# Attention and two gated layers on one core: first batch's exponentials head by head on ACT, pooled q and k by products, 32-bit low words, and a table of urgencies for the list schedule

## The chip, the core and the metric

The kernel runs on one core of one Trainium2 chip. The core has a matrix engine (PE, whose weight loads are shown apart as PEld), a vector engine (DVE), a scalar engine (ACT), a general engine (POOL), and a queue engine (SP) that issues every transfer of this kernel. Each works through its own instructions in order, and semaphores join them. The metric is the time of one execution in microseconds, as the median of several runs.

## The reference

Four batches with 8 heads, 576 positions and 64 values a head go through two attentions that are added: a pooled one, in which q, k and v are averaged over groups of 4 positions, and a local one, in which a position sees its neighbours up to distance 3. The sum, as 2304 tokens of 512 values, goes through a product of two projections and a third one, and then through a layer with a leaky rectifier whose slope is `alpha`:

```
q_d = q.reshape(B, H, Sd, 4, D).mean(axis=3)          # k_d, v_d alike
out_up = repeat(sm_attn(q_d, k_d, v_d), 4)
mask = abs(pos[:, None] - pos[None, :]) < 4
out_local = softmax(where(mask, scale * q @ k.T, -1e9)) @ v
x = tokens(out_up + out_local)
x = (x @ w_a) * (x @ w_b) @ w_out
h = x @ w_in;  return (maximum(h, 0) + alpha * minimum(h, 0)) @ w_out2
```

q, k and v are 32-bit floats; the five weight matrices come as 64-bit floats.

## The kernel before

**Attention.** The tokens are cut into 24 tiles of 96 (`TQ`), six to a batch. For a tile, `turn` transposes q and k on PE (four transposes of 128 columns each into one bank of PSUM), ACT copies them to SBUF (`zone`), and DVE sums groups of four columns of the copy into the pooled q and k of the batch (`gq_z`, `gk_z`). `soft` makes the scores of 8 heads in two banks (4 heads, 416 columns each), and per bank DVE takes the maximum of each row and head (`nm`), and subtracts it while it writes the scores to SBUF; then one ACT instruction makes the exponentials of all 832 columns, DVE sums them per head (`nz`), inverts the sums and multiplies. `p_turn` transposes the result, `av_t` multiplies by v, `x_add` adds the pooled attention and splits x into two 16-bit parts (`xt`). `g_top`, `g_minus`, `g_exp` and `g_out` are the pooled attention of a batch; it needs the pooled q and k of all six tiles.

**Weights.** `narrow` makes 32-bit floats out of 64-bit ones, in halves: ACT scales the low word down and writes it into the low 16 bits of the place it was read from, DVE masks the 16 bits above, DVE shifts the high word into the destination, POOL adds the two. Then the weights are scaled and split into two 16-bit parts by ACT and DVE (`wab` for w_a and w_b, `wo` for w_out, and in `zone`, once attention is over, w_in and w_out2).

**Dense layers.** `s1` (24 PE instructions of 288 columns in two groups of 12; then ACT, DVE, ACT, DVE), `s2`, `s3` and `s4` are the dense products. They form the list `chain`, whose order on PE is fixed.

**Order.** The class `Plan` records every operation with a modelled duration (`cost`), and `schedule` lays them out: of the operations that are ready on an engine, the one with the highest `prio` goes first, which is the modelled length of what hangs on it plus a `bias` given by hand for its group (a tile, a chunk of weights, a block). `fill` then puts idle products of an identity matrix (`m<-idf`, 256 columns) into the gaps that PE has by that plan up to 200 us: a number that covers 0.7 of the gap. The names `turn3`, `soft3`, `wab1`, `s1_0_5` are the groups. So a change of costs or biases moves operations on all engines, and the number of fills with them. In the trace nearly everything has the line L269 (the helper that issues), so groups are told by operation and tile.

Of the kernel before, what the change touches and what calls it, by code (L numbers as in the profile page):

```python
# [12 lines left out]
U32 = mybir.dt.uint32  # L13
I64 = mybir.dt.int64
ACTF = mybir.ActivationFunctionType
ALU = mybir.AluOpType
AX = mybir.AxisListType
# [8 lines left out]
class Plan:  # L26
# [66 lines left out]
    def cost(self, eng, method, out, ins, kw):  # L93
        n = self.free(out)
        if eng == self.PE:
            if method == "transpose":
                n = self.free(out)
                w = 2 if ins[0].dtype == F32 else 1
            else:
                w = 4 if ins[0].dtype == F32 else 1  # L100
            return max(0.03, n * w * 0.000425)
        m = max([n] + [self.free(a) for a in ins])
        if eng == self.POOL:
            return 0.2 + m * (0.0026 if method == "tensor_tensor" else 0.0011)
        if eng == self.ACT:
            if ins and ins[0].dtype == U32:
                return 0.2 + 0.00243 * m
            return 0.2 + 0.0009 * m + (0.19 if kw.get("accum_out") is not None else 0)
        if out.dtype == I16:
            return 0.1 + 0.00144 * m  # L110
        if method in ("tensor_scalar", "tensor_copy", "memset", "tensor_scalar_mul"):
            return 0.12 + 0.0009 * m
        return 0.14 + 0.0011 * m
# [79 lines left out]
    def schedule(self, chain):  # L193
        for a, b in zip(chain, chain[1:]):
            b.preds.add(a)
        for o in self.ops:
            for p in o.preds:
                p.succ.append(o)
        for o in reversed(self.ops):
            t = 0.0  # L200
            for s in o.succ:
                t = max(t, s.tail + self.lat(o, s))
            d = o.dur + (sum(o.dma) if o.dma else 0.0)
            o.tail = t + d
            o.prio = max([o.tail + o.bias] + [s.prio + self.lat(o, s) + d for s in o.succ])
            o.left, o.est = len(o.preds), o.free
        ready = {e: [] for e in (self.PE, self.DVE, self.ACT, self.POOL, self.SP)}
        free = dict.fromkeys(ready, 0.0)
        self.dma_free = 0.0
        for o in self.ops:  # L210
            if not o.left:
                ready[o.eng].append(o)
        order = []
        while True:
            best = None
            for e, lst in ready.items():
                if lst:
                    t = max(free[e], min(o.est for o in lst))
                    if best is None or t < best[0]:
                        best = (t, e)  # L220
            if best is None:
                break
            t, e = best
            o = max((o for o in ready[e] if o.est <= t + 1e-9), key=lambda o: (o.prio, -o.n))
            ready[e].remove(o)
            o.start, free[e] = t, t + o.dur
            o.end = free[e]
            if o.dma:
                self.dma_free = max(self.dma_free, t + 0.5) + o.dma[0]
                o.end = max(o.end, self.dma_free + o.dma[1])  # L230
            order.append(o)
            for s in o.succ:
                s.est = max(s.est, o.end + self.lat(o, s))
                s.left -= 1
                if not s.left:
                    ready[s.eng].append(s)
        assert len(order) == len(self.ops)
        self.order = order
        return order
# [36 lines left out]
def kernel(  # L276
# [17 lines left out]
    P = Plan(nc)  # L294
# [3 lines left out]
    def T(method, *a, **kw):  # L298
        P("tensor", method, *a, **kw)

    def V(method, *a, **kw):
        P("vector", method, *a, **kw)

    def A(method, *a, **kw):
        P("scalar", method, *a, **kw)

    def G(method, *a, **kw):
        P("gpsimd", method, *a, **kw)
# [18 lines left out]
    TQ = 96  # L327
    WK = 104
    TPB = S // TQ
# [4 lines left out]
    TP = TQ // FAC  # L334
    H2 = H // 2
    XR = 3 * N1
    scale = 1.0 / float(D) ** 0.5
# [12 lines left out]
    def bank(tag):  # L350
        nbank[tag] += 1
        return banks[tag][(nbank[tag] - 1) % len(banks[tag])]
# [80 lines left out]
    cal = []  # L433
# [26 lines left out]
    def narrow(raw, dst):  # L460


        w = raw.bitcast(I32).rearrange("p (n t) -> p n t", t=2)
        h = raw.bitcast(I16).rearrange("p (n t) -> p n t", t=4)
        A("activation", out=h[:, :, 0], in_=raw.bitcast(U32).rearrange("p (n t) -> p n t", t=2)[:, :, 0],
          func=ACTF.Copy, scale=2.0 ** -29)
        V("tensor_scalar", out=h[:, :, 1], in0=h[:, :, 3], scalar1=-0x4000, scalar2=None, op0=ALU.bitwise_and)
        d = dst.bitcast(I32)
        V("tensor_scalar", out=d, in0=w[:, :, 1], scalar1=3, scalar2=0x3FFFFFFF,
          op0=ALU.logical_shift_left, op1=ALU.bitwise_and)  # L470
        G("tensor_tensor", out=d, in0=d, in1=w[:, :, 0], op=ALU.add)
# [60 lines left out]
    pool_m = const.tile([WK, 3, 120], F32, name="pool_m")  # L532
# [25 lines left out]
    def raw_of(i):  # L558
        r = raw_t(i)
        return (r[:TQ, :H * D], r[:, H * D:2 * H * D], r[:, 2 * H * D:].rearrange("p (h d) -> p h d", h=H))  # L560
# [37 lines left out]
    def win(i):  # L598
        b, t = divmod(i, TPB)
        s0 = t * TQ  # L600
        kb = min(max(s0 - 4, 0), S - WK)
        return b, s0, kb, s0 - kb


    sm = {}

    def load(i, js=(0, 1, 2)):
        b, s0, kb, off = win(i)
        t = raw_of(i)
        for j in js:  # L610
            src, r0, n = ((q, s0, TQ), (k, kb, WK), (v, kb, WK))[j]
            dma(t[2] if j == 2 else t[j].rearrange("p (h d) -> p h d", h=H),
                src[b, :, r0:r0 + n, :].rearrange("h p d -> p h d"))

    def turn(i, tag):

        b, s0, kb, off = win(i)
        rq, rk, _ = raw_of(i)
        qz, kz = qk_of(i)
        t = i % TPB  # L620
        for src, n, dst, acc, o in ((rq, TQ, qz, gq_z[b % 2], 0), (rk, WK, kz, gk_z[b % 2], off)):
            ps = bank(tag)[:, :H2 * n].rearrange("p (a n) -> p a n", a=H2)
            with pe():
                for p in range(H2):
                    T("transpose", ps[:, p], src[:, p * 128:(p + 1) * 128], idf[:n, :n])
            A("copy", dst, ps)
            V("tensor_reduce", out=acc[:, :, t * TP:(t + 1) * TP],
              in_=dst[:, :, o:o + TQ].rearrange("p a (n r) -> p a n r", r=FAC), axis=AX.X, op=ALU.add)

# [10 lines left out]
    def p_of(i):  # L640

        return raw_t(i)[:TQ, :H * WK].rearrange("p (h n) -> p h n", h=H)

    def soft(i, tag="a"):

        qz, kz = qk_of(i)
        m, z = (ring(f"n{x}", [TQ, H]) for x in "mz")
        pss = [bank(tag)[:TQ, :H2 * WK].rearrange("p (h n) -> p h n", h=H2) for _ in range(2)]
        p = p_of(i)
        with pe():  # L650
            for ps in pss:
                T("matmul", ps, idb[:TQ, :TQ], mask[:, win(i)[3] // 4].unsqueeze(1).to_broadcast([TQ, H2, WK]),
                  start=True, stop=False)
            for h in range(H):
                T("matmul", pss[h % 2][:, h // 2], qz[rows(h), h // 2], kz[rows(h), h // 2], start=False,
                  stop=(h >= H - 2))
        for g in range(2):
            hs = slice(H2 * g, H2 * g + H2)
            V("tensor_reduce", out=m[:, hs], in_=pss[g], axis=AX.X, op=ALU.max)
            V("tensor_tensor", out=p[:, hs], in0=pss[g], in1=m[:, hs].unsqueeze(2).to_broadcast([TQ, H2, WK]),  # L660
              op=ALU.subtract)
        A("activation", out=p, in_=p, func=ACTF.Exp, scale=scale)
        V("tensor_reduce", out=z, in_=p, axis=AX.X, op=ALU.add)
        V("tensor_scalar_add", z, z, 1e-9)
        V("reciprocal", z, z)
        V("tensor_tensor", out=p, in0=p, in1=z.unsqueeze(2).to_broadcast([TQ, H, WK]), op=ALU.mult)
# [419 lines left out]
    for f in range(F1):  # L1086
        c, e = divmod(f, FPC)
# [28 lines left out]
    for n, i in enumerate((3, 4, 5)):  # L1116
        t = head_end + 4 * n
# [8 lines left out]
    for b in range(1, B):  # L1126
        for t in range(TPB):
            i = b * TPB + t
            ti = first[b] + pace[b] * t
            bias = lead[b] + spread[b] * (TPB - t)  # L1130
# [15 lines left out]
    for i in range(3, NTILE):  # L1146
        b, t = divmod(i, TPB)
# [27 lines left out]
    for j in range(NBLK):  # L1175
# [6 lines left out]
        for t in range(NB // 128):  # L1182
            on(n0 + 31.6 + 10.3 * t, lambda j=j, t=t: s4(j, t), f"s4_{j}_{t}")

    cal.sort(key=lambda x: x[:2])
    for _, _, fn, P.name, P.bias, P.rel in cal:
        fn()
    P.schedule(chain)
    ib = idf.bitcast(BF16)
# [33 lines left out]
```

## Time and profile before

| | |
|---|---|
| runs | 1040.88, 1047.79, 1048.54 us, median 1047.79 |
| the profiled execution | 1049.7 us, of which the span from the first to the last instruction is 1047.4 |
| PE busy | 1011.8 us (97%), of which 53.4 us are fills |
| DVE busy | 599.8 us (57%) |
| ACT busy | 506.8 us (48%) |
| POOL busy | 133.7 us (13%) |
| mean granted clock of PE | 0.984 |

A row of the page gives an engine's busy time, its share of the span and its instructions. A busy PE is not always useful: the fills count as busy, and two records stand for one product of 32-bit floats. What bounds the kernel has to be read stretch by stretch.

### The profile page before, as it was taken

To read this page: it belongs to the slowest core of one execution; us is meant where nothing else is said; L and a number is where in the kernel's file an instruction comes from. 1 tells how busy PE (TensorE), PEld (TensorE's weight loads), DVE (VectorE), ACT (ScalarE), POOL (GpSimd) and SP (SyncE) were. 2 spreads that over 40 slices of the span, in tenths; PEclk is the share of its full clock that TensorE was granted. 3 is DMA by queue.
4 is the path that set the end of the run, shared out by engine and by line. 5 is a ranking of instruction groups with operands and counts; after the bars stand their busy time and mean duration, and the time that the engine had idled before them with its cause. 6 is when DMAs were issued, how large, how long until landed. Compare 5 with 4: busy or idle time off the path is not lost.

```text
span 1047.4 us, 18866 instructions
## 1 busy us (share of the span) xinstructions
PE 1011.8 (97%) x7749; PEld 701.3 (67%) x7749; DVE 599.8 (57%) x1247; ACT 506.8 (48%) x955; POOL 133.7 (13%) x128
## 2 busy tenths in 40 slices
PE   8889799989999999999988999999999999999998
PEld 5677677768787787887866777754645545454553
DVE  5899998847655567473998577450513315142240
ACT  3677688533433434253766666460624417153350
POOL 2335640001100012000253210000000000000000
PEclk9889999989999999999999999999999999999999
DMA  9674641014310144111661411010010100100000
GB/s 160 226 209 144 163 134 26 1 25 72 72 48 1 48 75 91 24 64 41 205 196 55 151 42 35 13 32 21 11 46 16 41 21 8 66 12 11 21 1 30
DMA packets 95942, 69.50 MB, mean 66 GB/s; under 512 B 71152, under 2 KB 78704, under 8 KB 95856
## 3 DMA queue, kind: packets, MB, share of 16 engines
q1 hardware_dynamic: 95856, 68.31, 24.6%
q8 instruction: 60, 0.98, 0.4%
q14 instruction: 26, 0.21, 0.1%
HBM read 58.86 MB, written 9.44 MB: 65 GB/s over the span
## 4 chain that ended last, share of the span: by engine, by line
PE 84%; DVE 10%; SPq 2%; ACT 2%; issue 1%; DMA 1%; DVEq 0%; ACTq 0%
PE m L269 73%; PE a L269 10%; DVE zone L269 3%; SPq L269 2%; DVE wo L269 2%; DVE wab L269 1%; PE r L269 1%; ACT zone L269 1%; DMA zone<-in_v_dram 1%; DVE nz L269 1%; DVE xt L269 1%; ACT wo L269 0%; DVE gt L269 0%; DVE gm L269 0%; DVE tm L269 0%
## 5 line engine op out<-in xcount | busy, mean ns | idle before, releaser
L269 PEld LDWEIGHTS <-wab 128*128 128x128 f16 x3168 | 306.8, 98 | 166.4 <-issue 10.1
L269 PE MATMUL m<-xt,wab 128*128 128x288 f16 x2304 | 295.6, 286 | 8.0 <-DVE x2s L269 3.9
L269 PE MATMUL m<-xt,zone 128*128 128x384 f16 x1152 | 188.2, 326 | 0.0
L269 PE MATMUL m<-zone,wab 128*128 128x512 f16 x864 | 187.7, 379 | 0.0
L269 DVE SCALAR_TENSOR_TENSOR gt<-tm,nal,tm 128x384 f32<-128x384 f32 x96 | 59.3, 618 | 218.6 <-ACT tm L269 218.6
L269 PEld LDWEIGHTS <-zone 128*128 128x128 f16 x1152 | 112.7, 98 | 74.9
L269 ACT ACTIVATE tm<-m 128x384 f32<-128x384 f32 (+1 forms) x224 | 97.8, 478 | 112.1 <-PE m L269 112.1
L269 PEld LDWEIGHTS <-wo 128*128 128x128 f16 x1152 | 112.0, 99 | 31.2 <-issue 2.7
L269 POOL TENSOR_TENSOR zone<-zone 72x256 f32<-72x256 f32 (+2 forms) x60 | 75.5, 1266 | 393.7 <-DMA zone<-in_v_dram 220.2
L269 PE MATMUL m<-gt,wo 128*128 128x288 f16 x864 | 114.1, 290 | 0.4 <-DVE gt L269 0.3
L269 ACT ACTIVATE zone<-zone 96x832 f32<-96x832 f32 (+4 forms) x69 | 78.2, 1144 | 35.7 <-DVE zone L269 28.3
L269 PE MATMUL a<-zone 64*96 64x104 f32 (+3 forms) x1232 | 86.7, 269 | 4.7 <-DVE zone L269 3.8
L269 ACT ACTIVATE gt<-m,uf 128x512 f32<-128x512 f32 x18 | 12.4, 688 | 157.1 <-PE m L269 157.1
L269 PEld LDWEIGHTS a<-zone 64*96 64x96 f32 (+3 forms) x1232 | 71.3, 154 | 22.7 <-issue 13.6
L269 ACT COPY zone<-a 104x384 f32<-104x384 f32 (+3 forms) x112 | 50.0, 484 | 38.2 <-PE a L269 37.7
L269 ACT COPY tm<-m 128x288 f32<-128x288 f32 x96 | 38.4, 400 | 56.4 <-PE m L269 51.7
L269 DVE SCALAR_TENSOR_TENSOR tm<-m,tm 128x288 f32<-128x288 f32 x96 | 43.5, 453 | 37.7 <-PE m L269 27.6
L269 DVE SCALAR_TENSOR_TENSOR wab<-gt,kap,wab 128x384 f16<-128x384 f32 x96 | 58.8, 612 | 6.3 <-ACT wab L269 6.3
L269 ACT ACTIVATE wab<-gt,kap 128x384 f16<-128x384 f32 x96 | 59.1, 616 | 1.1 <-DVE gt L269 1.1
L269 PE MATMUL m<-idf 128*128 128x256 bf16 x377 | 53.4, 293 | 0.0
L269 ACT ACTIVATE gt<-tm 128x288 f16<-128x288 f32 x72 | 31.6, 442 | 40.8 <-DVE tm L269 40.8
L269 DVE TENSOR_SCALAR zone<-zone 128x512 int16<-128x512 int16 (+3 forms) x48 | 45.0, 964 | 4.2 <-ACT zone L269 3.9
(166 smaller groups left out, 933.3 us busy)
## 6 DMA issues: line engine op xcount, KB each, us to landing
zone<-in_moe_w_in_dram SPq DMA_DIRECT2D x8, 1024.0 KB
zone<-in_moe_w_out_dram SPq DMA_DIRECT2D x16, 512.0 KB
wo<-in_moe_w_a_dram SPq DMA_DIRECT2D x6, 1024.0 KB
wo<-in_moe_w_b_dram SPq DMA_DIRECT2D x6, 1024.0 KB
x_d<-x2s SPq DMA_DIRECT2D x8, 576.0 KB
out_dram<-gt SPq DMA_DIRECT2D x18, 256.0 KB
zone<-in_k_dram SPq DMA_DIRECT2D x21, 208.0 KB
zone<-in_v_dram SPq DMA_DIRECT2D x21, 208.0 KB
```

Source lines behind the costliest of these rows:

```text
L269: f(*args, **kw)
```

## The change

Five edits:

- In `narrow`, ACT writes the low word as 32 bits instead of 16; DVE's write of the upper 16 bits follows as before. The planner's cost of this operation goes from 2.43 to 1.2 ns an element.
- For the tiles of batch 0 (`i < 1 * TPB`) `soft` no longer subtracts on DVE: DVE multiplies the maxima by `-scale`, and ACT reads the scores from PSUM, eight instructions of 104 columns for a tile, each with the maximum as its bias and with the sum of its exponentials as a second result. DVE's sum over the tile goes.
- For batches 0 and 1 (`EARLY = 2`) `turn` no longer sums groups of four on DVE: after the four transposes PE multiplies the same columns by a matrix of ones (`pool_m`, 24 columns), into the rest of the same bank, and ACT copies the 96 columns of sums.
- Every group gets a number from the table `URGENT` on top of its bias.
- The schedule's second half becomes a method of its own, with no effect on the order.

```
@@ Plan.cost
             if ins and ins[0].dtype == U32:
-                return 0.2 + 0.00243 * m
+                return 0.2 + 0.0012 * m
@@ narrow
-        A("activation", out=h[:, :, 0], in_=raw.bitcast(U32).rearrange("p (n t) -> p n t", t=2)[:, :, 0],
+        A("activation", out=w[:, :, 0], in_=raw.bitcast(U32).rearrange("p (n t) -> p n t", t=2)[:, :, 0],
           func=ACTF.Copy, scale=2.0 ** -29)
@@ turn
-            ps = bank(tag)[:, :H2 * n].rearrange("p (a n) -> p a n", a=H2)
+            full = bank(tag)
+            ps = full[:, :H2 * n].rearrange("p (a n) -> p a n", a=H2)
+            sums = full[:, H2 * n:H2 * (n + TP)].rearrange("p (a n) -> p a n", a=H2)
+            early = b < EARLY
             with pe():
                 for p in range(H2):
                     T("transpose", ps[:, p], src[:, p * 128:(p + 1) * 128], idf[:n, :n])
+                if early:
+                    for p in range(H2):
+                        T("matmul", sums[:, p], src[:, p * 128:(p + 1) * 128], pool_m[:n, o // 4, 48:48 + TP],
+                          start=True, stop=True)
             A("copy", dst, ps)
+            if early:
+                A("copy", acc[:, :, t * TP:(t + 1) * TP], sums)
+                continue
             V("tensor_reduce", out=acc[:, :, t * TP:(t + 1) * TP],
@@ soft
             V("tensor_reduce", out=m[:, hs], in_=pss[g], axis=AX.X, op=ALU.max)
-            V("tensor_tensor", out=p[:, hs], in0=pss[g], in1=m[:, hs].unsqueeze(2).to_broadcast([TQ, H2, WK]),
-              op=ALU.subtract)
-        A("activation", out=p, in_=p, func=ACTF.Exp, scale=scale)
-        V("tensor_reduce", out=z, in_=p, axis=AX.X, op=ALU.add)
+            if i < 1 * TPB:
+                V("tensor_scalar_mul", m[:, hs], m[:, hs], -scale)
+                for h in range(H2):
+                    c = H2 * g + h
+                    A("activation", out=p[:, c], in_=pss[g][:, h], func=ACTF.Exp, scale=scale, bias=m[:, c:c + 1],
+                      accum_out=z[:, c:c + 1])
+            else:
+                V("tensor_tensor", out=p[:, hs], in0=pss[g], in1=m[:, hs].unsqueeze(2).to_broadcast([TQ, H2, WK]),
+                  op=ALU.subtract)
+        if i >= 1 * TPB:
+            A("activation", out=p, in_=p, func=ACTF.Exp, scale=scale)
+            V("tensor_reduce", out=z, in_=p, axis=AX.X, op=ALU.add)
@@ end of the kernel
+    URGENT = {"alphas": 35, "bs0": -45, "bs1": -5, "gexp0": -70, "gexp1": -5, "gexp2": 25, "gexp3": -50,
...
-    for _, _, fn, P.name, P.bias, P.rel in cal:
+    for _, _, fn, P.name, bias, P.rel in cal:
+        P.bias = bias + URGENT.get(group(P.name), 0.0)
         fn()
```

Counted over the whole program, the fills go from 377 to 334, 96 products with `pool_m` come in, 24 of the 48 sums of four on DVE go, with 12 subtractions and 6 sums of exponentials, and 12 small multiplications come in.

**DVE, third tile.** These rows of DVE stand in the first part of the program, around the softmax of tile 2, whose scores lie in the banks `a_69` and `a_67` and whose exponentials lie in `x2s`; `wab<-wo` and `wo<-wo` are steps of `narrow`. Before:

```order
L269 TENSOR_REDUCE nm_125<-a_69 96x4
L269 COPY gt_135<-a_68 24x144
L269 TENSOR_TENSOR x2s<-a_69,nm_125 96x416
L269 TENSOR_REDUCE nm_125<-a_67 96x4
L269 TENSOR_REDUCE tr_119<-r_70 2x1
L269 TENSOR_TENSOR x2s<-a_67,nm_125 96x416
L269 TENSOR_SCALAR td_121<-idf,tr_119 2x2
L269 TENSOR_SCALAR wab<-wo 128x1024
```

and now:

```order
L272 TENSOR_REDUCE nm_125<-a_69 96x4
L272 COPY gt_135<-a_68 24x144
L272 TENSOR_SCALAR nm_125<-nm_125 96x4
L272 TENSOR_REDUCE nm_125<-a_67 96x4
L272 TENSOR_SCALAR wab<-wo 128x1024
L272 TENSOR_SCALAR nm_125<-nm_125 96x4
L272 TENSOR_REDUCE tr_119<-r_70 2x1
```

The two subtractions are gone, two multiplications of 4 columns stand in their place, and a step of `narrow` has moved up between them.

**ACT, the same tile.** These rows of ACT stand around the exponentials of tile 2; `wo<-wo` is the low word of a chunk of weights, `zone<-a` with 72 rows is `g_exp` of batch 0. Before:

```order
L269 ACTIVATE wo<-wo 128x1024
L269 ACTIVATE zone<-a_68 72x432
L269 ACTIVATE x2s<-x2s 96x832
L269 ACTIVATE zone<-a_69 72x432
L269 ACTIVATE wo<-wo 128x1024
L269 ACTIVATE zone<-a_67 72x432
```

and now:

```order
L272 ACTIVATE wab,wm_117<-wab 128x1024
L272 ACTIVATE x2s,nz_127<-a_69,nm_125 96x104 x4
L272 ACTIVATE x2s,nz_127<-a_67,nm_125 96x104 x4
L272 ACTIVATE wo<-wo 128x1024
L272 ACTIVATE zone<-a_68 72x432
L272 ACTIVATE zone<-a_69 72x432
```

One instruction has become eight, they read PSUM, and they now stand ahead of `g_exp` of batch 0.

**PE, a tile of batch 1.** These rows of PE stand where the `s1` groups (`m<-xt,wab`) already follow each other; `a<-idf,zone` are the transposes of a tile's k (104 columns) and q (96). Before:

```order
L269 MATMUL a_68<-idf,zone 128x104 x4
L269 MATMUL a_67<-idf,zone 128x96 x4
```

and now:

```order
L272 MATMUL m_65<-xt,wab 128x288
L272 MATMUL a_68<-zone 64x96 x8
L272 MATMUL a_67<-idf,zone 128x104 x4
L272 MATMUL a_67<-pool_m,zone 128x24 x4
L272 MATMUL a_69<-idf,zone 128x96 x4
L272 MATMUL a_69<-pool_m,zone 128x24 x4
```

Behind each four transposes stand four products of 24 columns. Of the twelve such fours of batch 1, two stand ahead of the last long rows of fills and ten behind them. Behind the eighth group of 12 products of `s1`, 30 of the fills stood in the program, and 17 do now.

## Rows read from the trace of the kernel before

**Rows 1.** The page: busy us, share of the span, instructions.
```profile
PE 1011.8 (97%) x7749; PEld 701.3 (67%) x7749; DVE 599.8 (57%) x1247; ACT 506.8 (48%) x955; POOL 133.7 (13%) x128
```

**Rows 2.** Busy time by stretch: stretch, us, PE, PEld, DVE, ACT, POOL, clock, DMA share, GB/s.
```profile
0.00:26.70 26.70, 21.90 (x169) 15.48 (x169) 15.73 (x36) 9.93 (x18) 7.79 (x44) 1.00 0.99 164
26.70:120.60 93.90, 79.45 (x730) 63.17 (x731) 87.45 (x144) 63.91 (x76) 43.70 (x21) 0.87 0.64 186
120.60:200.00 79.40, 79.27 (x744) 63.18 (x744) 70.75 (x164) 59.37 (x116) 21.06 (x16) 1.00 0.28 75
200.00:240.00 40.00, 35.81 (x315) 27.39 (x313) 21.86 (x57) 15.62 (x30) 0.00 (x0) 0.87 0.08 17
240.00:505.00 265.00, 265.00 (x2527) 212.00 (x2526) 164.00 (x392) 102.74 (x219) 21.22 (x25) 1.00 0.27 59
505.00:640.00 135.00, 126.73 (x1017) 99.28 (x1015) 108.92 (x222) 94.36 (x164) 39.96 (x23) 1.00 0.35 114
```

**Rows 3.** Instruction groups of PE: the fills in 26.7:120.6, then in 120.6:200.
```profile
L269 PE MATMUL m<-idf 128*128 128x256 bf16 x296 | 40.6, 293 | 0.0
...
L269 PE MATMUL m<-idf 128*128 128x256 bf16 x30 | 4.1, 273 | 0.0
```

**Rows 4.** The chain of work, 20 to 120 us: start, length, what.
```profile
20.63 6.08 DMA zone<-in_v_dram
...
30.05 2.41 ACT wo L269
...
117.88 1.26 ACT wo L269
...
120.56 5.92 PE m L269 x47
```

**Rows 5.** Instruction groups of DVE in 26.7:120.6 (busy, mean ns); the last in the whole run.
```profile
L269 DVE TENSOR_SCALAR wo<-wo 128x1024 int16<-128x1024 int16 x12 | 16.3, 1359 | 0.1
L269 DVE TENSOR_SCALAR wab<-wo 128x1024 int32<-128x1024 int32 x12 | 9.8, 817 | 0.0
L269 DVE TENSOR_TENSOR zone<-a,nm 96x416 f32<-96x416 f32 x8 | 4.3, 579 | 0.0
L269 DVE TENSOR_REDUCE nz<-zone 96x8 f32<-96x832 f32 x3 | 3.0, 989 | 0.0
L269 DVE TENSOR_REDUCE zone<-zone 128x96 f32<-128x384 f32 x2 | 1.1, 538 | 0.0
...
L269 DVE TENSOR_SCALAR nz<-nz 96x8 f32<-96x8 f32 x24 | 6.0, 249 | 0.1
```

**Rows 6.** Instruction groups of ACT: six in 26.7:120.6, the last two in the whole run.
```profile
L269 ACT ACTIVATE wo<-wo 128x1024 int16<-128x1024 uint32 x12 | 30.1, 2505 | 0.0
L269 ACT ACTIVATE wab<-wab 128x1024 bf16<-128x1024 f32 x6 | 6.3, 1053 | 7.0 <-DVE wab L269 5.0 <-POOL wab L269 2.0
L269 ACT ACTIVATE x2s<-x2s 128x512 int16<-128x512 uint32 x3 | 4.1, 1372 | 0.0
L269 ACT ACTIVATE zone<-zone 96x832 f32<-96x832 f32 x4 | 3.6, 893 | 0.5 <-DVE zone L269 0.4
L269 ACT ACTIVATE xt<-zone,sx 128x384 f16<-128x384 f32 x5 | 2.9, 612 | 0.1
L269 ACT ACTIVATION_READ_ACCUMULATOR wab<-wab 128x1 f32 x6 | 1.1, 188 | 0.0
...
L269 ACT ACTIVATE tm<-m 128x384 f32<-128x384 f32 x192 | 84.3, 488 | 63.1 <-PE m L269 63.1
L269 ACT COPY zone<-a 128x288 f32<-128x288 f32 x8 | 3.2, 399 | 7.8 <-PE a L269 7.5
```

**Rows 7.** The chain of work at 137 and 236 us: small 32-bit products on PE.
```profile
137.49 0.31 PE r L269 x2
...
236.28 2.07 PE a L269 x32
```

**Rows 8.** The chain of work at 540 us, and PE's longest wait in 505:640.
```profile
540.80 3.00 ACT zone L269 x3
...
544.04 2.42 ACT zone L269
...
PE m L269 <- DVE x2s L269: 3.9, 3, 2.3
```

**Rows 9.** The chain of work around 230 us: groups of 12 products of `s2`.
```profile
224.49 3.00 PE m L269 x12
...
234.81 1.47 PE m L269 x12
```

More of the change, by code (lines that the diff above doesn't have):

```diff
@@ L198, in schedule, with reschedule @@
                 p.succ.append(o)
+        return self.reschedule()
+    def reschedule(self):
         for o in reversed(self.ops):
@@ L605 @@
     sm = {}
+    EARLY = 2
     def load(i, js=(0, 1, 2)):
@@ L1183, with group @@
             on(n0 + 31.6 + 10.3 * t, lambda j=j, t=t: s4(j, t), f"s4_{j}_{t}")
+    def group(name):
+        kind = name.rstrip("0123456789")
+        n = name[len(kind):]
+        if kind in ("turn", "bound", "soft", "pturn", "av", "v", "x", "load") and n:
+            b = int(n) // TPB
+            return f"{kind}@{b}" if kind in ("x", "load") else f"t@{b}" if b else f"t0@{n}"
+        if name[:3] in ("s1_", "s2_"):
+            return f"{name[:2]}@{name[3]}"
+        return kind if kind in ("wow", "wos", "wo2w", "wo2s") else name
+    URGENT = {"alphas": 35, "bs0": -45, "bs1": -5, "gexp0": -70, "gexp1": -5, "gexp2": 25, "gexp3": -50,
[12 rows of a table added]
     cal.sort(key=lambda x: x[:2])
-    for _, _, fn, P.name, P.bias, P.rel in cal:
+    for _, _, fn, P.name, bias, P.rel in cal:
+        P.bias = bias + URGENT.get(group(P.name), 0.0)
         fn()
```

12 rows, old and new, of the table URGENT are left out of this document.

## The prediction

> **What bounds the kernel now.** The page comes first [rows 1]: PE is busy 97% of the span. That says that PE ends most of the time, not that it works: 53.4 us are fills, and 1047.4 - 1011.8 = 35.6 us are idle. So I read the stretches next [rows 2], and in each ask who has no time left. From 240 to 505 us PE is busy all 265 us: nothing that DVE or ACT saves there shows, and each product that PE gets shows in full. The same holds from 120.6 to 200 (79.27 of 79.40). From 26.7 to 120.6 it is otherwise: DVE is busy 87.45 of 93.90 us, and PE's 79.45 hold 40.6 us of fills [rows 3]. The chain of waits agrees: up to 26.7 us it hangs on the load of v [rows 4], from there to 120.56 us, where the first long row of `s1` begins, it is DVE nearly throughout, with two low words of `narrow` on ACT in it (2.41 and 1.26 us). From 505 to 640 PE lacks 135.0 - 126.7 = 8.3 us; it waits for DVE most [rows 8], and the chain goes through ACT for 3.00 and 2.42 us there, low words again.
>
> So there are two currencies. Up to 120 us a microsecond of DVE is worth about one, behind that one of PE is.
>
> **The change, part by part.** *Softmax of batch 0.* In the stretch that DVE bounds lie the tiles 2 to 5. Eight subtractions at 579 ns [rows 5] go (4.6 us) and four sums of exponentials at 989 ns (4.0 us); eight small multiplications come. The nearest row to these is an operation on 8 columns, at 249 ns: 2.0 us. Tiles 0 and 1 lie ahead of 26.7 us, where the load of v decides and DVE is busy 15.73 of 26.70 us [rows 2]: nothing.
>
> *Pooled q and k, on DVE.* Two of the 24 sums of four lie in that stretch (538 ns each, 1.1 us, [rows 5]). Twelve lie ahead of it and the other ten behind it, beside a busy PE: nothing. So DVE's stretch gets shorter by 4.6 + 4.0 + 1.1 - 2.0 = **7.7 us**. The bounds: nothing, if another engine takes DVE's place, and some 12 us if the new order also moves DVE's work behind the first `s1`.
>
> *Pooled q and k, on PE.* 96 products come in. 56 of them stand among fills and cost nothing as long as fills stand around them, else their own time. Forty, ten fours, stand in the `s1` rows, where PE has no time left. The trace has no 32-bit product of 24 columns with 128 weight columns. From below I take 32 records in 2.07 us [rows 7], two records a product (72 weight columns, 65 columns moved): 0.13 us. From above a lone product with 128 weight columns and one or two columns moved, 0.31 us, with PE's start on it. Four in a row share a start, so I take 0.17, nearer to the lower row: 40 x 0.17 = **6.8 us later** (5.2 to 12.4).
>
> The Trainium skill has a rule for this: TensorE: Matmul & The Clock Gate, section LDWEIGHTS, lets a load of weights last as many cycles of 1.2 GHz as it has columns, 107 ns for 128. By it a product with two loads would cost 0.21 us, forty 8.5 us, and the sum below would come out 1.7 us later. No run here shows such a product yet.
>
> *ACT's part.* A head's exponentials: 288 columns take 399 ns and 832 take 893 [rows 6], so 104 take about 0.23; an operand by partition adds 612 - 488 = 0.12, the sum read out 0.19: 0.54 us, or 0.44 where neighbours overlap. Eight take 3.5 to 4.3 us, against 0.9. For four tiles in the stretch ACT gets 10 to 14 us more. It had 30 us idle there [rows 2], so this costs nothing on the path while ACT is not late; the last small sum of a tile does come 2.6 to 3.4 us later, and what waits for it on DVE are the reciprocal and the product of the tile, behind which DVE has steps of `narrow` to do.
>
> *Low words.* Sixteen lie in the stretch, 12 of 1024 words at 2505 ns (30.1 us, [rows 6]) and four of 512 at about 1370. Why they are slow the trace does not tell: the same ACT writes 1024 16-bit results side by side in 1053 ns; a 16-bit write at a step of 8 bytes costs DVE 1359 ns against 817 for a 32-bit one side by side [rows 5]; and this is the only ACT row that reads unsigned words. Between no gain and 1053 I take half, about 1.3 us. Most of that is beside the path; on it are 2.41 + 1.26 us [rows 4], halved: **1.8 us** gained (0 to 2.2). From 505 to 640 us half of 5.4 us would be 2.7; DVE, which is waited for there, gains nothing by it, so I take **1.5** (0 to 2.7).
>
> *The order.* It shows 13 fewer fills behind the eighth `s1` group, where PE is the bound. A fill there takes 4.1 / 30 = 0.137 us [rows 3]: **1.8 us** gained. The other thirty that go stand where DVE decides: nothing. The stall of `s1` from 505 to 640 has the same DVE work in front of it in the new order, a little earlier and more spread; I count nothing for that, with 8.3 us as its end. From 200 to 240 us the operations stand as before; nothing.
>
> *The sum.* -7.7 + 6.8 - 1.8 - 1.5 - 1.8 = **-6.0 us**. The profiled execution has 1047.4 us of span and 2.3 around it, 1049.7, and would become 1043.7. It lies 1.9 us above the median of the three runs, 1047.79, which are 0.7% apart among themselves. From the median the same sum gives **1041.8 us**.
>
> **The rivals.** *More comes out of it (1026 to 1036).* The table puts DVE's work in an order in which the first `s1` comes the full 12 us earlier, and the stall at 505 to 640 goes (8.3 us), with products at the lower price: -12 - 8.3 - 1.8 - 1.8 + 5.2 = -18.7, **1029**. For it: both stalls are waits behind DVE operations that could stand later, and the subtractions read PSUM while POOL adds. Against it: DVE's sum up to 640 us falls by little more than the terms above.
>
> *ACT takes DVE's place (slower).* The low words are no faster, and ACT gets 17 us of exponentials (32 x 0.54) less 3.6 and some 1 us of copies: 63.9 + 14.7 = 78.6 us in a stretch in which DVE then has 87.45 - 7.7 = 79.8. From there on both engines are full and wait for each other at each tile: the reciprocal stands behind eight exponentials, and these behind a low word of 2.5 us. At 3.4 us a tile, four tiles pay 13.6: -7.7 + 13.6 + 6.8 - 1.8 = +10.9, **1058.7**. It decides as soon as a low word of 1024 stays above about 2.2 us. For it: nothing in the rows says that the width of the write is what is slow. The Trainium skill speaks for it too: SBUF — State Buffer, section Door 1, lets a step cost nothing as long as two accesses fall into one line of 16 bytes, and a step of 8 bytes does so with 16 bits as with 32. Against that page stands DVE's row, dearer at just that step.
>
> *PE pays more behind 120 us (slower).* Products at 0.31 us are 12.4 us. And PE's clock can fall beside small products: a group of 12 of `s2` took 3.00 us at 224 us, 1.47 at 234 [rows 9], in a stretch with a granted clock of 0.87 [rows 2], after waits and small 32-bit products. If 10 us between 120 and 200 went at 1.2 GHz, 5 us would be lost: -7.7 + 12.4 + 5 - 5.1 = +4.6, **1052**.
>
> *The head does not get shorter:* the loads or POOL's adds (43.7 us in the stretch) set the pace once DVE does not; then the pace of `s1` stays and only PE's terms count: 6.8 - 1.8 = +5.0, less 1.5: **1051**.
>
> **How the numbers follow.** About 1% (10.5 us) is what runs that are 0.7% apart can tell from no change; so faster means below 1037.3, slower above 1058.3. Forecast, 1035 to 1048: 0.46. More comes out of it: 0.26. ACT takes DVE's place: 0.12, PE pays more: 0.09, the head stays: 0.07. Faster: 0.26 and a fifth of the forecast, 0.36. Slower: half of ACT's case and a third of PE's, 0.09, and 0.03 for both at once: 0.12. The rest, 0.52, is within 1%. The range is 1027 to 1056: it leaves out 0.09 below, where more comes out of it than worked out, and 0.1 above.
>
> **What would show each step.** DVE's subtractions of batch 0 gone and its stretch up to the first long row of `s1` 6 to 9 us shorter: the start of that row near 111 us. The low word of 1024 near 1.3 us; at 2.5 ACT's busy share up to there rises above 80%, and DVE, which had no idle time, waits for ACT. The products of 24 columns: a four in 0.5 to 0.9 us between two `s1` groups, and PE's busy time without fills up by 14 to 20 us. From 505 to 640 us, PE's idle time of 8.3 us down to about 7, or to nothing in the first rival. The prediction is wrong if the first `s1` row begins as before, if it begins earlier than 105 us, or if a product with `pool_m` takes over 0.3 us.

## The result, and the profile after

| | median, us | runs, us | ratio to before, 95% interval |
|---|---|---|---|
| before | 1047.38 | 1040.88 to 1048.54 | |
| changed | 1058.76 | 1056.42 to 1060.74 | 1.0117 [1.0098, 1.0137] |

Slower by 11 us, where 6 us less was forecast and 1056 was the range's upper end. The profiled execution took 1057.83 us, of which the span is 1056.1. The page's row of busy times, to set beside [rows 1]:

```profile
PE 1030.2 (98%) x7898; PEld 722.6 (68%) x7898; DVE 586.0 (55%) x1217; ACT 478.3 (45%) x1069; POOL 142.0 (13%) x128
```

PE is busy 18.4 us longer and idle 9.7 us less: the kernel is longer by the difference. The same stretches as in [rows 2] (stretch, us, PE, PEld, DVE, ACT, POOL, clock, DMA share, GB/s):

```profile
0.00:26.70 26.70, 22.35 (x120) 18.82 (x121) 4.01 (x13) 7.07 (x27) 7.73 (x44) 1.00 1.00 166
26.70:120.60 93.90, 80.94 (x775) 63.65 (x773) 79.22 (x141) 55.32 (x155) 46.26 (x20) 0.95 0.56 167
120.60:200.00 79.40, 78.57 (x700) 65.63 (x701) 65.78 (x120) 50.71 (x115) 25.16 (x17) 0.91 0.37 96
505.00:640.00 135.00, 133.78 (x1088) 105.41 (x1087) 106.92 (x220) 74.94 (x159) 39.48 (x23) 1.00 0.39 126
```

Up to 26.7 us DVE has 4.01 us of work where it had 15.73: it waits for PE. From 505 to 640 us the stall of 8.3 us is down to 1.2. The chain of waits (start, length, what), which in [rows 4] ran over the load of v, DVE and ACT to 120.56 us:

```profile
19.95 9.23 PE m L272 x57
...
33.63 10.46 PE m L272 x69
...
50.56 2.24 DVE wo L272
...
115.06 5.21 issue
...
124.41 6.17 PE a L272 x40
...
134.87 9.47 PE m L272 x77
```

Up to 49 us it is PE nearly throughout. The last piece starts with five fills; on PE's timeline the first long row of `s1` stands here, before and after:

```profile
120.56 5.92 PE L269 MATMUL m<-xt,wab 128*128 128x288 f16 x47 [0.77 <-DVE xt L269]
```
```profile
135.36 8.98 PE L272 MATMUL m<-xt,wab 128*128 128x288 f16 x72
```

It begins 14.8 us later than before, where a start near 111 us was forecast. Where the difference lies along the run is seen from the start of the blocks of `s2` (a block's first row on PE's timeline; the order of these products is the same in all kernels):

| start of `s2`, us | block 0 | 1 | 4 | 6 | span |
|---|---|---|---|---|---|
| before | 210.7 | 297.5 | 465.2 | 595.2 | 1047.4 |
| changed | 233.5 | 315.4 | 485.0 | 605.3 | 1056.1 |
| changed, without products | 214.1 | 294.8 | 464.4 | 584.6 | 1035.4 |
| changed, products in batch 0 alone | 224.5 | 307.9 | 477.5 | 597.7 | 1048.6 |
| changed, without the table | 234.5 | 317.9 | 485.5 | 614.7 | 1066.9 |
| changed, 12 fills ahead (c_warm) | 224.3 | 307.6 | 477.1 | 597.4 | 1048.2 |

Some 18 us are lost ahead of block 1, 20 by block 4, and about 10 of them come back from there to block 6.

### The profile page after: what moved, and what is told of

The parts are those of the page before. It is cut to its first block, busy times and chain, and to the rows that moved or that the text cites. A ratio compares the mean times of both kernels' runs of the same rounds, so it can differ in the third digit from the quotient of the medians.

```text
span 1056.1 us, 19258 instructions
## 1 busy us (share of the span) xinstructions
PE 1030.2 (98%) x7898; PEld 722.6 (68%) x7898; DVE 586.0 (55%) x1217; ACT 478.3 (45%) x1069; POOL 142.0 (13%) x128
## 4 chain that ended last, share of the span: by engine, by line
PE 90%; DVE 8%; issue 1%; ACT 1%; POOL 0%; DVEq 0%; POOLq 0%; ACTq 0%
PE m L272 78%; PE a L272 11%; DVE wo L272 1%; DVE zone L272 1%; PE r L272 1%; DVE wab L272 1%; DVE gt L272 1%; DVE nm L272 1%; DVE gm L272 0%; DVE td L272 0%; DVE x2s L272 0%; ACT zone L272 0%; DVE gn L272 0%; DVE ws L272 0%; DVE xt L272 0%
## 5 line engine op out<-in xcount | busy, mean ns | idle before, releaser
L272 POOL TENSOR_TENSOR zone<-zone 72x256 f32<-72x256 f32 (+2 forms) x60 | 81.6, 1369 | 389.5 <-DVE zone L272 126.7
L272 PE MATMUL a<-zone 64*96 64x104 f32 (+3 forms) x1232 | 83.9, 264 | 2.0 <-DVE zone L272 1.3
L272 PEld LDWEIGHTS a<-zone 64*96 64x96 f32 (+3 forms) x1232 | 68.6, 150 | 19.9 <-issue 13.4
L272 ACT COPY zone<-a 104x384 f32<-104x384 f32 (+4 forms) x124 | 51.5, 458 | 42.4 <-PE a L272 42.1
L272 ACT ACTIVATE zone<-zone 96x832 f32<-96x832 f32 (+4 forms) x66 | 54.3, 826 | 25.1 <-DVE zone L272 21.1
L272 PE MATMUL m<-idf 128*128 128x256 bf16 x334 | 50.9, 309 | 0.0
L272 DVE SCALAR_TENSOR_TENSOR gt<-gt,tm 128x288 f16<-128x288 f16 x72 | 46.4, 649 | 6.6 <-ACT gt L272 6.2
```

Of the source, the lines that this page charges most:

```text
L272: f(*args, **kw)
```

## Experiments: parts taken out of the changed kernel

The theory after the two traces was that the products hold PE; the rivals were the table's order and the clock. Kernels of one group share their runs of before (median 1045.27 in this one). A time is followed by its ratio to before and the 95% interval; 0.002 of ratio is 2 us. A "four" is the four products behind four transposes.

**a_noprod**: `-    EARLY = 2`, `+    EARLY = 0`.

> The changed kernel, with the pooled q and k of all four batches summed on DVE again (EARLY = 0); low words, exponentials by head and table stay. Theory P (products): the 48 products of batch 0 hold PE 13.9 us between 5 and 44 us, narrow begins at 43.4 us behind them instead of 30.0, and so the first long s1 row at 134.9 instead of 120.6; the forty in the s1 rows cost 0.21 us each. Then narrow begins near 30 us, the first long s1 row at 118 to 122 us, and the time falls by some 14 + 8.3 us to 1036 to 1040. Rival T (table): the table puts attention ahead of narrow, whatever PE does; then the first long row stays at 130 or later and only the 8.3 us of the s1 rows come back: 1049 to 1052.

1038.81 us, 0.9935 [0.9911, 0.9958]: as theory P has it, 20 us below the changed kernel. The first step of `narrow` on DVE, in the changed kernel and without products:

```profile
43.35 0.68 DVE L272 TENSOR_SCALAR wab<-wo 128x1024 int32<-128x1024 int32 x1
```
```profile
28.79 0.68 DVE L272 TENSOR_SCALAR wab<-wo 128x1024 int32<-128x1024 int32 x1
```

The first long row, though, is at 123.9 us, 2 us behind theory P's range and still not ahead of before: that part of the forecast fails without products too.

**a_early1**: `+    EARLY = 1`.

> The changed kernel, with products for batch 0 alone (EARLY = 1); batch 1 is summed on DVE. This takes the forty products out of the s1 rows and leaves the head's 48. Theories P and T agree: the head stays as it is in the changed kernel (first long s1 row at 133 to 136 us), and PE gets 40 x 0.21 = 8.4 us back behind it: 1050 to 1051. If a product costs the 0.17 us of the forecast in truth and something else slows the rows: 1052. If the time stays at 1057 or more, PE's time in the s1 rows isn't what ends the kernel.

1050.30 us, 1.0029 [1.0012, 1.0047], as both theories have it. The 48 products of batch 1 cost 8.5 us (1058.76 - 1050.30), those of batch 0 another 11.5 (1050.30 - 1038.81). The split is less sure than the sum of 20: the ten runs here range from 1046.37 to 1051.76. In the table above the first difference is constant from block 1 on (7.5 us), and so is the second (13.1 us): both are lost early and nothing behind gives them back. A product's price is read from a tile's piece in the chain of waits, before (24 instructions) and after (16 records of products more):

```profile
130.08 1.65 PE a L269 x24
```
```profile
146.48 3.35 PE a L272 x40
```

(3.35 - 1.65) / 8 = 0.21 us.

**a_notable**: the table's numbers left out.

```
-        P.bias = bias + URGENT.get(group(P.name), 0.0)
+        P.bias = bias
```

> The changed kernel without the table of urgencies (its numbers are all 0); products, low words and exponentials by head stay. Theory P: PE's products hold the head as before, narrow begins at 40 us or later and the first long s1 row at 130 us or later; from 505 to 640 us the stall of 8.3 us comes back at least in part, so 1058 to 1066. Rival T: the head is that of the kernel before, the first long s1 row near 121 us, and the time 1043 to 1050.

1069.20 us, 1.0225 [1.0199, 1.0251], 10 us above the changed kernel and 3 above theory P's range; the head is as theory P has it. Up to block 4 it is late by 0.5 to 2.5 us, at block 6 by 9.4. So the table isn't what costs the head; it is what removed the stall. From 505 to 640 us PE is busy here

```profile
505.00:640.00 135.00, 129.23 (x1065) 101.65 (x1064) 100.75 (x196) 71.87 (x155) 39.92 (x23) 0.97 0.40 126
```

**a_cost**: the planner is told a product's time.

```
                 w = 4 if ins[0].dtype == F32 else 1
+                if n == 24 and w == 4:
+                    return 0.21
```

> The changed kernel, whose planner counts a product of 24 columns as 0.21 us (it counts 0.041 now). The program then has 273 fills in place of 334, 32 of the 61 that go ahead of the first s1. Theory P: PE's queue in the head gets 32 x 0.137 = 4.4 us shorter, and narrow is laid in the time in which DVE waits: first long s1 row at 125 to 131 us, 1049 to 1055. Rival C (clock): PE works at its lower level up to about 24 us since products stand where fills stood, and with fewer fills still it rises later: transposes of 96 columns at 0.9 us a four up to 30 us or later, and the time stays at 1056 to 1061.

1053.35 us, 1.0068 [1.0045, 1.0092]: theory P. `narrow` begins at 35.41 us and the first long row at 123.7. So 5.4 us of the products' price come from a plan that counts 0.16 us for four of them.

## Experiments: parts put into the kernel before

Median of before: 1045.67 us. Each is the changed kernel with `EARLY = 0` and the other parts set back.

**b_low**: the 32-bit write and its planner cost alone.

> The kernel before with the 32-bit low words alone (and their planner cost of 1.2 ns an element); softmax, sums of four and biases are those of before. By the forecast's terms (1.8 us in the head, 1.5 from 505 to 640) 3.3 us below the kernel before, and up to 4.5 now that a low word of 1024 is seen to take 1.17 us and not the 1.3 of the forecast. Theory H (the head isn't bound by ACT): nothing in the head, 0 to 3 us from 505 to 640.

1036.06 us, 0.9904 [0.9885, 0.9924]: 9.6 us faster, three times the forecast, and `s2` begins at 199.7 us: most of it lies in the head. Neither number was right.

**b_exp**: batch 0's exponentials by head alone.

> The kernel before with the exponentials of batch 0 head by head on ACT alone; low words stay 16-bit at 2.5 us, sums of four stay on DVE, biases are those of before. By the forecast's term (4.6 + 4.0 - 2.0 of DVE in its stretch) 6.6 us below the kernel before. Theory H: DVE's stretch also holds waits behind POOL's additions (a step of xt of 0.6 us shown as 3.93 us, ending with an addition), so that DVE's savings go into longer waits: within 2 us of before. Rival A (ACT takes DVE's place): with low words at 2.5 us ACT is full, 5 to 11 us above before.

1048.73 us, 1.0034 [1.0016, 1.0052]: 3 us slower, as none of the three has it.

**b_lowexp**: both.

> The kernel before with both the 32-bit low words and the exponentials of batch 0 by head, without products and without the table. By the forecast's terms 9.9 us below before. With a table that costs the head what products don't (theory T for the head): the first block of s2 begins at 203 to 206 us, 7 us or so ahead of 210.7 in before. Theory H: it begins at 209 to 213 us, and the time is 0 to 4 us below before, all of it from 505 to 640 us.

1043.23 us, 0.9964 [0.9946, 0.9983]. The exponentials cost the low-words kernel 7.2 us: the sign of the forecast's largest term is wrong.

**b_lowtable**: low words and table.

> The kernel before with the 32-bit low words and the table; no products, exponentials as before. Beside the changed kernel without products (1038.8 us) it differs by the exponentials alone. If those save DVE 6.6 us on the path: 1045. Theory H: they save nothing, 1036 to 1041, and the gain over before lies behind 465 us, as the table took 10.8 us out of the changed kernel there.

1031.77 us, 0.9859 [0.9844, 0.9875], the fastest kernel here: 1.4% under before, 2.5% under the changed one, and below both forecasts. The table gives 4.3 us on top of the low words, and the exponentials would cost 7.0 here too (a_noprod). From before over b_low, b_lowtable, a_noprod and a_early1 to the changed kernel the steps are -9.6 - 4.3 + 7.0 + 11.5 + 8.5 = +13.1. That is one path from end to end, so the sum has to come out (the ratio says +12) and does not show that the parts are independent. They are not: the exponentials cost 3 us alone and 7 beside the new low words.

## Experiments: clock, tiles, and half a table

Median of before: 1046.58 us.

**c_warm**: 12 fills at the start.

```
+    n = next(n for n, o in enumerate(P.order) if o.calls[0][0] == nc.gpsimd.affine_select)
+    o = P.new(P.PE)
+    o.calls = [(nc.tensor.matmul, (banks["m"][2][:, :256], ib[:, :128], ib), dict(start=True, stop=True))] * 12
+    P.order.insert(n + 1, o)
```

> The changed kernel with 12 fills of the identity (256 columns) at the very start of PE's work, ahead of the first transposes; everything else and its order stay. Theory C: that PE works at its lower level up to 24 us in the changed kernel (five fours of products at 1.6 us each instead of 0.83, transposes 0.9 us a four instead of 0.5) and only to 11 us in the kernel before comes from products standing where fills stood; more fills ahead bring the rise forward to some 10 to 15 us, 5 to 6 us of the head come back, 1052 to 1055. Theory N: the rise doesn't hang on a few fills; fours at 1.6 us up to 24 us as before, and the 12 fills, which take the place of idle time up to 4.4 us, change nothing or cost 1 us: 1058 to 1061.

1049.95 us, 1.0065 [1.0034, 1.0096]; of nine runs five lie at 1048.7 to 1050.0 and four at 1056.8 to 1058.8, so the gain does not come every time. PE's timeline of the changed kernel (start, length, what):

```profile
5.07 1.78 PE L272 MATMUL m<-pool_m,gt 104*128 104x24 f32 x8
...
17.87 0.93 PE L272 MATMUL m<-idf,x2s 104*128 104x104 f32 x4
18.60 1.78 PE L272 MATMUL m<-pool_m,x2s 104*128 104x24 f32 x8
...
26.41 0.52 PE L272 MATMUL m<-idf,zone 104*128 104x104 f32 x4
26.77 0.99 PE L272 MATMUL m<-pool_m,zone 104*128 104x24 f32 x8
```

and with the 12 fills ahead:

```profile
1.83 2.74 PE L272 MATMUL m<-idf 128*128 128x256 bf16 x12 [1.83 <-POOL idf L272]
4.59 0.81 PE L272 MATMUL m<-idf,gt 104*128 104x104 f32 x4
5.24 0.99 PE L272 MATMUL m<-pool_m,gt 104*128 104x24 f32 x8
```

The same four products take 1.78 us up to 20 us in the one and 0.99 from 5 us on in the other. Theory C holds for these two executions, and the price is 9 us of head (first long row at 126.2), more than the 5 to 6 expected. In the table, block 1 of `s2` comes back by 7.9 us, of the 20.7 by which all the products had moved it.

**c_exp35**, **c_exp02**: a_noprod with `if TPB // 2 <= i < TPB:` and with `if i < TPB // 2:` in `soft`.

> The changed kernel without products, with exponentials by head for tiles 3 to 5 alone; tiles 0 to 2 subtract on DVE as before. In the run without products (1038.8 us) and in the one with low words and exponentials, DVE runs narrow back to back behind the softmax of tile 2, an addition of POOL lasts 7.9 us there (2.4 alone), and DVE then waits 4.2 us for a load of w_a that is issued behind it; with the old softmax neither is seen, and the time is 7.0 us less. Theory S (that one place): with tile 2 as before, the wait is gone and 4 to 5 of the 7 us come back: 1033 to 1035. Theory E (each tile pays, ACT's eight instructions hold the banks): half comes back, 1035 to 1036.5. By the forecast (each such tile gains): above 1038.

> The changed kernel without products, with exponentials by head for tiles 0 to 2 alone; tiles 3 to 5 subtract on DVE as before. Theory S: the long addition behind tile 2 and the wait of 4.2 us for the load of w_a stay: 1036 to 1039. Theory E: half of the 7 us, 1035 to 1036.5. If this one is at 1032 to 1034 and tiles 3 to 5 are those that pay, the wait for the load isn't what costs.

1044.09 us, 0.9982 [0.9970, 0.9994], and 1035.11 us, 0.9884 [0.9853, 0.9915]. Both theories miss c_exp35. Theory S falls with the other: c_exp02 keeps the wait and loses little in the head (block 1 of `s2` at 288.1 us, 288.5 in b_lowtable).

```profile
DVE wab L272 <- DMA wo<-in_moe_w_a_dram: 4.2, 1, 4.2
```

Tiles 0 to 2 pay about 3 of the 7 us, as theory E has it, but tiles 3 to 5 pay 12: with another set of durations the list is another everywhere (c_exp35 has 130.06 of 135.00 us of PE busy from 505 to 640, a_noprod 133.80). So single parts had to be tried in an unchanged order.

**c_latetable**: b_lowtable with the numbers of batch 0, `wab`, `wo` and `s1` blocks 0 and 1 left out.

> The kernel before with 32-bit low words and a table cut to the groups behind the first batch (the numbers of batch 0's attention, of wab, wo and of s1 blocks 0 and 1 are 0). With the whole table the first block of s2 begins at 206.2 us and the time is 1031.8; without a table it begins at 199.7, and the time is 1036.1. If the table's gain lies behind 300 us alone and its cost ahead of 200 us, both halves add: s2 at 199 to 201 us, 1025 to 1028. If the order in the head and the late order hang together (batch 1 moves into the time that the head gives): 1031 to 1037.

1037.41 us, 0.9911 [0.9883, 0.9939]: at the upper end of the second case. `s2` begins at 201.4 us, but the late gain is gone: the halves don't add.

## Experiments: one part, every other instruction in its old place

Medians of before: 1046.01 and, for the last two, 1046.21 us.

**d_lowfrozen**: before with the 32-bit write, the planner's cost left at 2.43 ns.

> The kernel before with the 32-bit write of the low words alone, and the planner's old cost of 2.43 ns an element kept, so that every engine's instructions stand in the order of the kernel before. The version with the new cost came out 9.6 us faster, where the forecast had 3.3. Theory W (the write itself): ACT's low word gates the additions and so the loads, whatever the order; 1037 to 1040. Theory O (the order): the planner, told the shorter cost, lays narrow earlier, and that is most of it; in the old order 1042 to 1045.

1044.28 us, 0.9988 [0.9972, 1.0004]: theory O. The write alone gives 1.7 us, which these runs do not tell from nothing; some 8 of b_low's 9.6 us come from the order that the planner lays once it knows the shorter time.

**d_expfrozen**, **d_expfrozen_table**: b_low's and b_lowtable's plan, in which only the calls are exchanged (`nm` times `-scale` for the subtraction, eight exponentials for one, nothing for the sum).

> The kernel with the 32-bit low words alone (1036.1 us), in its order instruction for instruction, but with batch 0's subtractions replaced by the small multiplications, its six long exponentials by eight short ones each that read PSUM, and its six sums left out. The version in which the planner orders them anew came out 7.2 us slower. Theory O (the new order costs it): in the old order at least nothing is lost and up to the forecast's 6.6 us gained: 1030 to 1036. Theory E (the engines: ACT's 3.3 us a tile come late, the two banks are held longer, POOL's additions stretch): 1040 to 1044 in the old order too.

> The same on the kernel with low words and table (1031.8 us), in its order instruction for instruction. Planned anew, the exponentials by head cost it 7.0 us. Theory O: 1025 to 1032. Theory E: 1036 to 1040.

1042.70 us, 0.9969 [0.9949, 0.9989], against 1036.06; and 1034.13 us, 0.9883 [0.9861, 0.9905], against 1031.77. In no order is anything gained; in one 6.6 us are lost, in the other 2.4, which is within the intervals: theory E in the first, between the theories in the second. In the first, over 26.7 to 100 us, DVE's busy time goes from 70.20 to 67.22 us only. Two things stand in the trace. DVE's groups of b_low, then of d_expfrozen (busy, mean ns):

```profile
L272 DVE TENSOR_TENSOR zone<-a,nm 96x416 f32<-96x416 f32 x8 | 4.3, 573 | 0.0
```
```profile
L272 DVE TENSOR_SCALAR nm<-nm 96x4 f32<-96x4 f32 x8 | 5.4, 699 | 0.0
```

A multiplication of four columns takes more on average than a subtraction of 416, of which it replaces one; one that waits for nothing takes 0.15 (at 46.08 us). And what DVE waits for ACT (us, times, longest), 26.7 to 120.6 us, was 0.7 us in b_low and is

```profile
DVE xt L272 <- ACT xt L272: 3.1, 2, 1.6
DVE zone L272 <- ACT zone L272: 0.7, 1, 0.7
DVE nz L272 <- ACT zone L272: 0.6, 1, 0.6
```

4.4 us in all: in ACT's queue a step of `xt` stands behind eight exponentials (96.42 to 99.02 us).

**e_mulact**, **e_mulact_table**: the same two, with the maxima of a tile multiplied on ACT.

```
-                P.ops[-1].calls = [(nc.vector.tensor_scalar_mul, (m[:, hs], m[:, hs], -scale), {})]
+                P.ops[-1].calls = []
...
+            P.ops[-1].calls = [(nc.scalar.activation, (), dict(out=m, in_=m, func=ACTF.Copy, scale=-scale))] + [
```

> As the kernel with the exponentials by head in the unchanged order of the low-words kernel (1042.7 us, against 1036.1 with the old softmax), but the maxima of a tile are multiplied on ACT, 8 columns at once, and no longer by two instructions on DVE. Everything else stands instruction for instruction. In five traces these multiplications, from SBUF to SBUF, lasted on average 1.4 us longer in all 8 cases in which they began beside an addition of POOL, while the subtractions that they replace, which read PSUM, lasted longer in none of 9. Theory M (the multiplication waits for POOL, and the second maximum and the tile behind it): without it 1034 to 1038. Theory A (ACT's eight instructions come too late for DVE): 1041 to 1045.

> The same in the order of the kernel with low words and table (1031.8 us with the old softmax, 1034.1 with exponentials by head and the multiplication on DVE). Theory M: 1028 to 1032. Theory A: 1033 to 1037.

1038.69 us, 0.9929 [0.9909, 0.9949], 4.0 below d_expfrozen; and 1036.43 us, 0.9908 [0.9888, 0.9929], 2.3 above d_expfrozen_table, which the intervals do not tell from nothing. The first lies just above theory M's range, the second in theory A's. DVE's waits for ACT rise from 4.4 to 5.6 us in the first, and from 5.3 to 6.7 in the second (none in b_lowtable). So neither wait alone explains both orders. That the two are the whole loss is not shown: the profiled execution of d_expfrozen took 1039.54 us, 3.1 more than that of b_low, so its waits bear on 3 of the 6.6 us between the medians. Nor were the banks tried apart, which are now held until ACT has read them: PE waits 1.4 us for exponentials in d_expfrozen (at 47.01 us), and not in b_low.

**d_lowtable_warm**: b_lowtable with the 12 fills.

> The kernel with low words and table (1031.8 us), with 12 fills of the identity ahead of the first transposes, which took 8.8 us off the changed kernel. There, PE had no idle time from 10 to 49 us; here the load of v sets the end of the first 27 us, and the transposes go at 0.5 us a four from 11 us on. If only a PE that is the bound gains: 1031 to 1033, though transposes are at 0.5 us a four from 5 us on. If the earlier rise helps here too: 1027 to 1029.

1032.05 us, 0.9866 [0.9850, 0.9882]: no gain. Where the load of v ends the stretch (in b_lowtable the chain of waits goes through it to 27.4 us), PE's pace in it is worth nothing.

## Why the prediction was wrong

Two steps failed.

**DVE's stretch is worth its length (-7.7).** The first is "a microsecond of DVE is worth about one". DVE's busy 87.45 us contained waits. Its timeline of the changed kernel, with POOL's beside it, in the place where the chain shows 5.21 us of "issue":

```profile
114.92 5.44 DVE L272 TENSOR_SCALAR us_ab<-us_ab 128x2 int32<-128x2 int32 x1
```
```profile
115.48 2.38 POOL L272 TENSOR_TENSOR wab<-wab,wo 128x1024 int32<-128x1024 int32 x1
117.81 2.52 POOL L272 TENSOR_TENSOR wo<-wo,x2s 128x512 int32<-128x512 int32 x2
```

An instruction on two columns is shown as 5.44 us and ends with POOL's additions. In the kernel before, what DVE's instructions show above the shortest of their form adds up to some 22 us between 26.7 and 120.6 us. [rows 5] has means only, in which this can't be seen; the timeline, row by row, would have shown it. In place of -7.7 the softmax of batch 0 measured +2.4 to +7.2 us, by the order that it stood in; the two sums of four (1.1 us of the term) were not tried apart. The multiplication's price of 249 ns was also a mean with such waits in it, and the subtraction that it replaces, which reads PSUM, is never seen to wait.

**Products among fills are free (0).** This is the second, and the largest single price: 11.5 us. Fills are instructions in PE's order like any other; a product does not take a fill's place when it runs longer than planned, it pushes everything behind it. Twelve fours took 13.9 us where the plan held 2.0, five of them at the lower pace. The condition stood in the prediction ("as long as fills stand around them"), and the new order's fills in that stretch (222 ahead of the first `s1`, not 237) should have been set against it. The pace is the larger part: in c_warm the same products stand in the same places, and at the faster pace the twelve fours take 10.0 us and the table's block 1 begins 7.9 us earlier. By that, some 8 of the 13.1 us that batch 0's products cost in the traces are PE's slower pace up to 20 us, of transposes and fills too, and some 5 are the products' own. The prediction looked for a slower PE behind 120 us alone.

**Products in the `s1` rows (+6.8).** Right in kind; a product takes 0.21 us and not 0.17, 8.5 us in all. The Trainium skill's rule, TensorE: Matmul & The Clock Gate, section LDWEIGHTS, gave 0.21, and the trace agrees with it to the hundredth at PE's faster pace; at the slower one a product takes 0.40 (1.6 us from one four's start to what follows it).

**ACT's part.** A head's exponentials begin 0.33 us apart, eight in 2.6 us, under the 3.5 to 4.3 worked out, and ACT is busy 55.32 of 93.90 us: it is not full, so the rival as put does not hold. Yet in d_expfrozen, where ACT is busy 56.91 of these 93.90 us, DVE waits for it 4.4 us: a queue in order makes others wait long before it is full.

**Low words (-3.3).**

```profile
L272 ACT ACTIVATE wo<-wo 128x1024 int32<-128x1024 uint32 x12 | 14.0, 1166 | 0.0
L272 ACT ACTIVATE x2s<-x2s 128x512 int32<-128x512 uint32 x8 | 5.4, 670 | 0.0
```

1166 ns against 2505 in [rows 6], a little better than half. The rival that reasoned from the Trainium skill, SBUF — State Buffer, section Door 1 (a step of 8 bytes costs nothing with 16 bits or 32) is thereby refuted for this write: it is the 16 bits that were slow. The write's own gain, 1.7 us in an unchanged order, is half of the forecast; the 8 us by the order were not in the sum at all.

**The order (-1.8, stall unchanged).** Mis-sized: the table gives 4.3 to 10.4 us, by removing the stall of 8.3 us that the forecast left standing. This is the first rival's condition, and it came true while the rest of that rival did not.

Of the rivals, PE paying more looked behind 120 us, where 8.5 us came. The clock fell there too, after PE had idled 3.94 us, and 3.09 us a little earlier: the granted clock, the last column but two, reads 0.50, the lower of its two levels, 1.2 GHz (1.00 in the same stretch before), and the piece of 40 took 6.17 us at 124 us and 3.35 at 146.

```profile
121.00:133.00 12.00, 11.57 (x67) 10.23 (x68) 9.20 (x13) 5.73 (x15) 7.50 (x4) 0.50 0.63 169
```

But the larger price lay ahead of 50 us. ACT's rival has nearly the right time (1058.7) by a cause that the rows refute: luck.

## What to carry to other kernels

Before a microsecond of an engine's busy time is counted as one of the path, compare each row with the shortest of its form: what lies above can be waiting, and work taken out is then waited for elsewhere. Work for an engine whose order is fixed costs its full time even among idle instructions, and a planner's cost that is wrong by a factor of five puts everything behind it in the wrong place. In a kernel whose order a planner lays out, change the planner's costs and the calls apart: here the order moved the time by 8 us where the faster instruction itself gave less than 2.

## What the chip showed that was not expected

**DVE and POOL.** In the traces of before, b_low, b_lowexp, a_noprod and d_expfrozen I counted, up to 200 us, the instructions that began beside an addition of POOL which would end at least 0.3 us after the shortest of their form would have: the multiplications of `nm` lasted over 0.3 us longer than that shortest one in 8 of 8 cases (1.4 us on average), those of `nz` in 9 of 11; the subtractions that read PSUM in none of 11, the maxima in none of 28, the reciprocals of `nz` in none of 11. A small instruction isn't spared. The Trainium skill, SBUF — State Buffer, section Who interferes with whom, says that an instruction of the kind of these multiplications can take a pair of ports that DVE shares with POOL and that whoever is first holds it to the end, while reductions never contend; these counts agree.

**The clock.** Twelve bf16 fills in 2.74 us of otherwise idle time, and fours of small 32-bit products run in 0.99 us from 5 us on; with the products first, PE was at work without a pause from 10 us on and the fours took 1.78 us until some 20 us. The column of the granted clock shows 1.00 for 0 to 26.7 us in both, so it does not tell the two apart; transposes of the same form do (0.93 and 0.52 us a four). That it is the clock is inferred from this ratio, and why the gain does not come every time stays open.
